# A channel-attention kernel: 47 streamed rows loaded at a later place of the first pass, and 48 others one step earlier

## The chip, the core and the metric

The kernel runs on one core of one Trainium2 chip. The metric is device time in microseconds (us), from the start to the end of one launch. The kernel before was run three times: 720.6, 721.79 and 721.95 us, median 721.79 us. One further execution was recorded by the hardware profiler; it took 720.55 us, and the span from its first to its last instruction is 718.7 us.

The engines are called by their short names: PE (TensorE, matrix products), DVE (VectorE), ACT (ScalarE), POOL (GpSimd), and SP (SyncE, which here only issues DMAs). DMA transfers move rows between HBM, the chip's main memory, and SBUF, the memory that the engines read.

## What is computed

```python
g = jnp.einsum("bhwc->bc", x) / (H * W)      # mean of every channel
gp = jnp.pad(g, ((0, 0), (pad, pad)))        # k = 1, so pad = 0
s = jnp.zeros_like(g)
for i in range(k):
    s = s + gp[:, i:i + C] * w1d[i]
s = _sigmoid(s)
return x * s[:, None, None, :]               # every pixel scaled by its channel's gate
```

`x` is 1 x 384 x 384 x 384 in bfloat16. Seen as pixels by channels that is 147456 x 384. With 128 partitions there are 1152 pixels to a partition; one "row" below is one pixel's 384 channels on each of the 128 partitions, 128 x 384 x 2 = 98304 bytes. The gates depend on all rows, so nothing can be scaled until the last row has been summed: the kernel reads x in a first pass, forms the gates, and writes the scaled x in a second pass.

## The kernel before, in words

**Where rows live.** SBUF holds one buffer, `arena`, of `ROWS` = 275 row slots. The letters in the code are slot numbers: `U` = 108, `G0` = 116, `V` = 212, `A` = 220, `W` = 232, `T` = 259, `Y` = 267. Slots `T` to the end are also the scratch space of the folding described below.

**Three kinds of rows.** Of the 1152 rows, 780 (`N_STREAM`) are *streamed*: loaded, summed, dropped, and loaded again in the second pass. The rest is kept from one pass to the next. 59 of these (`N_RAW`) stay in SBUF as they are; `take_raw` loads them last of all. The others come in *groups* (`GROUPS`): group 9 (`BANKED`) and group 0 (`FIRST`) at the very start, groups 1 to 8 of 32 rows each, and group 10 (`EXTRA`) of 16 rows. The groups are *folded*: four rows are packed into the space of three by placing bits of the fourth in the exponent fields of the other three (`fold`). A fold runs on DVE, with a range check on ACT between its two halves, and it overwrites the rows, so PE must have summed them before. It frees every fourth slot.

**First pass.** For each load SP issues one DMA (`load`, L255), and PE adds each of its rows into one accumulator with one matmul by a matrix of ones (`sum_rows`, issued at L261 or, for the first, at L275). The order is written out by hand: first pieces of up to 48 rows into the slots `EARLY`, with groups 1 and 3 between them, and then the list `BETWEEN`. An entry (g, slots) of it takes group g, folds it, and streams rows into the slots listed. For groups 6 to 8 the entry has two lists: the group comes in three loads of 12, 8 and 12 rows, the first list follows the fold of its first half and the second list the fold of its second half. After group 10 come the raw rows. A piece of over 40 rows in `BETWEEN` is preceded by 16 matmuls on zeros (`keep_warm`).

**What holds a load back.** SP works strictly in order. A load into a slot waits until the previous occupant has been summed by PE (or folded by DVE), and all later loads wait behind it. The class `Flow` derives these waits from the slots that each step reads and writes. The transfers that have already been issued go on meanwhile, in order. I call *lead* of a load the time by which its issue comes before the landing of the load issued just before it: it is the work that the DMA queue still had when SP added to it.

**Between the passes.** When PE has added the 1152nd row, ACT computes the gates (L474) and copies them (L478). Then DVE and POOL scale rows (L486), DVE unpacks the folded ones (L295, L301), SP issues the stores (L498) and, into the slots that come free, loads the streamed rows once more. The order of this second pass is made by a small planner at build time, from its own assumed costs and from the slots, group sizes and number of streamed rows; the lists of the first pass do not enter it.

Of the kernel before, what the change touches and what calls it, by code (L numbers as in the profile page):

```python
# [129 lines left out]
def kernel(  # L130
# [13 lines left out]
    B, H, W, C = x.shape  # L144
# [14 lines left out]
    U = 3 * PIECE + PAIRS * 3 * PAIR  # L159
    G0 = U + PAIR  # L160
    V = G0 + PAIRS * 3 * PAIR
    A = V + PAIR
    N_A = 39
    T = A + N_A
    Y = T + 2 * PIECE
# [12 lines left out]
    EXTRA = len(GROUPS)  # L178
    GROUPS.append((A, PIECE))
    W = A + 3 * PIECE  # L180
# [196 lines left out]
    def stream_all(where, n=None):  # L377
        i = 0
        n = sum(m for _, m in where) if n is None else n
        while n:  # L380
            a, m = where[i % len(where)]
            m = min(n, m)
            stream(m, a)
            n -= m
            i += 1
# [28 lines left out]
    S1, S2, S3 = ([slot] for slot in SLOTS)  # L414

    HIGH = [(A - 48, 48)]
    LOW_COLUMN = [(G0 - 48, 48)]
# [6 lines left out]
    def group(g, where):  # L424

        if isinstance(where, list):
            take(g)
            for k in of_group(g):
                fold(k)
            stream_all(where)  # L430
        else:
            k1, k2 = of_group(g)
            take(g, 0, 12)
            take(g, 24, 32)
            fold(k1)
            stream_all(where[0])
            take(g, 12, 24)
            fold(k2)
            stream_all(where[1])

    BETWEEN = [
        (2, LOW_COLUMN + [(A, 38)]), (4, HIGH),
        (5, [(G0 - 24, 24), (A - 24, 24)] + S1),
        (6, (S2, S3 + S1)), (7, (S2, S3 + S1)),
        (8, (S2 + S1, [(U, 8)] + S3)), (EXTRA, [(W + 4, 8)]),
    ]
    between = sum(n for _, b in BETWEEN for w in b for _, n in (w if isinstance(w, list) else [w]))
    first = N_STREAM - between
# [10 lines left out]
    folding = True  # L459
    for g, where in BETWEEN:  # L460
        group(g, where)
    assert streamed[0] == N_STREAM

    def take_raw(a, n):
        load(raw(a), a, n)
        sum_rows(a, n)

    for a, n in [(U, 8), (W + 12, 15), (V, 8), (W + 4, 8), (W, 4), (T, 8), (Y, 4), (Y + 4, 3), (Y + 7, 1)]:
        take_raw(a, n)
    assert summed[0] == RPP  # L470

# [250 lines left out]
    while True:  # L722

        if dve_at <= now:
# [4 lines left out]
            if landed and (ahead < PENDING or not can):  # L729
                a, at, n, end = landed.popleft()  # L730
# [13 lines left out]
        if alongside and alongside[0][0] <= now:  # L744
            _, a, at, n = alongside.popleft()
            store(at, a, n)
            moves.append([now + LAT, n * ROW + PER_STORE, stored(a, n)])
        while waiting and waiting[0][0] <= now:
            _, n, then, at, a, known = waiting.popleft()
# [12 lines left out]
        if bank_at is None and len(line) <= total - BANKS_AT and got and max(got)[0] >= N_BANKED:  # L762
            a = max(got)[1]
# [11 lines left out]
        if got and todo < N_STREAM:  # L775
            n, a = max(got)
            left = N_STREAM - todo
            left -= run_of(left - 1)[0]
            n = min(n, CAP, left)
# [54 lines left out]
```

## Time and profile before

| quantity | value |
|---|---|
| median of three runs | 721.79 us (720.6 to 721.95) |
| profiled execution | 720.55 us |
| its span | 718.7 us, so 1.85 us lie around it |
| first pass, to the end of the last row's sum | 269.65 us into the span |
| PE, DVE, ACT, POOL busy | 211.5, 485.8, 122.2, 10.2 us |
| DMA | 303.30 MB at a mean of 422 GB/s |

The profile's page divides the span into 40 equal slices of 18 us. In its rows of digits, 9 means 90% or more busy; the row PEclk is the clock granted to PE, in tenths of full speed. Other views are used beside the page. The chain of waits follows the work that ended last back to its start, and lists start, duration and what it was; a DMA in it runs from its issue to its landing. The table of stretches gives, for each stretch of time, its length, the busy time of each engine with the number of instructions in parentheses, then the granted clock, the share of the 16 DMA engines' time and the rate in GB/s. The timeline lists runs of equal instructions with start and duration and, in brackets, the idle time before them and what ended it. The view of one source line gives durations in ns, the start of the first and last instruction, and the time from a DMA's issue to its landing.

### The profile page before, as it was taken

What the parts mean: (1) busy time and instruction counts of PE and PEld (TensorE: products, weight loads), DVE (VectorE), ACT (ScalarE), POOL (GpSimd) and SP (SyncE); (2) the same over time, 40 slices, a digit from 0 to 9 for tenths busy, and PEclk for the clock granted to TensorE, in tenths of its full rate; (3) what the DMA queues carried; (4) which work ended last, traced back from release to release, by engine and by line L of the source; (5) the groups of instructions that cost most, each with busy time, mean ns of one, the idle gap of its engine ahead of it and who ended that gap; (6) DMA issues with size and microseconds to landing.
All of it is one profiled execution on the core that took longest, in us unless ns stands there. A gap on an engine that the chain in (4) does not pass through costs nothing.

```text
span 718.7 us, 2037 instructions
## 1 busy us (share of the span) xinstructions
PE 211.5 (29%) x1186; PEld 0.3 (0%) x3; DVE 485.8 (68%) x454; ACT 122.2 (17%) x101; POOL 10.2 (1%) x7
## 2 busy tenths in 40 slices
PE   4776978987987770000000000000000000000000
PEld 0000000000000000000000000000000000000000
DVE  4606270166789849999997999995991999105640
ACT  3604160144667630000002000000000000000000
POOL 0000000000000005000000000000000000000000
PEclk9998989999999995555555555555555555555555
DMA  9999999999999988999999999999999999999997
GB/s 371 444 428 435 434 429 428 438 431 428 409 428 426 427 353 342 411 425 433 425 434 428 433 435 444 434 420 445 417 447 423 427 448 421 449 427 426 439 425 317
DMA packets 20605, 303.30 MB, mean 422 GB/s; under 512 B 2290, under 2 KB 2674, under 8 KB 8306
## 3 DMA queue, kind: packets, MB, share of 16 engines
q1 hardware_dynamic: 20592, 303.18, 98.9%
q8 instruction: 4, 0.07, 0.0%
q14 instruction: 7, 0.06, 0.0%
q10 hardware_dynamic: 2, 0.00, 0.0%
HBM read 189.92 MB, written 113.25 MB: 422 GB/s over the span
## 4 chain that ended last, share of the span: by engine, by line
DMA 56%; DVE 25%; PE 7%; ACT 3%; another core or an unknown queue 2%; POOL 1%; SPq 1%; issue 0%; DVEq 0%; ACTq 0%
DMA arena<-in_x_dram 40%; DVE arena L486 17%; DMA out_dram<-arena 16%; PE bank L261 7%; DVE arena L295 5%; DVE arena L301 3%; ACT arena L332 2%; POOL arena L486 1%; SPq L255 1%; ACT arena L405 1%; SPq L498 0%; ACT s_bf L474 0%; ACT bank L478 0%; ACT bank L405 0%
## 5 line engine op out<-in xcount | busy, mean ns | idle before, releaser
L486 DVE TENSOR_TENSOR arena<-arena,s_bf 128x1536 bf16<-128x1536 bf16 (+9 forms) x100 | 231.1, 2344 | 78.5 <-DMA arena<-in_x_dram 67.5
L295 DVE TENSOR_SCALAR arena<-arena 128x1536 uint16<-128x1536 uint16 (+3 forms) x240 | 142.9, 644 | 118.6 <-DMA arena<-in_x_dram 101.8
L261 PE MATMUL bank<-arena,ones 128*128 128x384 bf16 x1151 | 205.6, 340 | 49.0 <-DMA arena<-in_x_dram 48.6
L332 ACT ACTIVATE arena<-arena 128x3072 uint16<-128x3072 uint16 (+1 forms) x40 | 108.0, 2699 | 107.7 <-DVE arena L295 107.7
L301 DVE TENSOR_TENSOR arena<-arena 128x1536 uint16<-128x1536 uint16 (+2 forms) x100 | 109.3, 1093 | 7.0 <-PE bank L261 3.1
L556 PE MATMUL bank<-odd,ones 128*128 128x1 bf16 x1 | 0.2, 185 | 313.6 <-DVE odd L551 313.6
L405 ACT COPY arena<-bank 128x512 uint32<-128x512 uint32 (+3 forms) x9 | 4.4, 497 | 106.7 <-DMA out_dram<-arena 106.5
L486 POOL TENSOR_TENSOR arena<-arena,s_bf 128x1536 bf16<-128x1536 bf16 (+1 forms) x3 | 10.0, 3350 | 270.2 <-ACT bank L478 270.2
L405 ACT COPY bank<-arena 128x512 uint32<-128x512 uint32 (+3 forms) x9 | 4.1, 493 | 35.6 <-PE bank L261 35.6
L486 DVE TENSOR_TENSOR arena<-arena,bank 128x1536 bf16<-128x1536 bf16 (+3 forms) x8 | 9.4, 1248 | 0.0
L332 ACT ACTIVATION_READ_ACCUMULATOR arena<-arena 128x1 f32 x40 | 7.5, 186 | 0.0
L261 PE MATMUL bank<-zeros,ones 128*128 128x384 bf16 x32 | 5.5, 326 | 0.0
L275 PE MATMUL bank<-arena,ones 128*128 128x384 bf16 x1 | 0.5, 479 | 7.2 <-DMA arena<-in_x_dram 7.2
L474 ACT ACTIVATE s_bf<-bank,w_sc 128x384 bf16<-128x384 f32 x1 | 0.6, 580 | 8.8 <-PE bank L261 8.8
L802 ACT ACT_TABLE_LOAD x1 | 1.3, 1283 | 0.7 <-PEq L818 0.7
L362 DVE TENSOR_SCALAR w_sc<-bank 128x1 f32<-128x1 f32 x1 | 0.2, 158 | 1.1 <-PE bank L357 1.1
L352 DVE MEMSET ones<- 128x128 bf16 x1 | 0.2, 165 | 1.0 <-SPq L107 1.0
L357 PE MATMUL bank<-w_bf,ones 1*128 1x1 bf16 x1 | 0.2, 179 | 2.1 <-DMA w_bf<-in_w1d_dram 2.1
L560 DVE CAST odd_i<-bank 128x1 int32<-128x1 f32 x1 | 0.2, 157 | 0.3 <-PE bank L556 0.3
L556 PEld LDWEIGHTS bank<-odd,ones 128*128 128x128 bf16 x1 | 0.1, 103 | 573.7 <-DVE odd L551 573.7
L478 ACT COPY bank<-s_bf 128x192 uint32<-128x192 uint32 x1 | 0.3, 323 | 0.0
L546 DVE TENSOR_REDUCE worst<-seen 128x1 f32<-128x40 f32 x1 | 0.2, 189 | 0.0
(8 smaller groups left out, 0.9 us busy)
## 6 DMA issues: line engine op xcount, KB each, us to landing
arena<-in_x_dram SPq DMA_DIRECT2D x17, 4608.0 KB, 29.9
out_dram<-arena SPq DMA_DIRECT2D x9, 3072.0 KB, 24.5
out_dram<-arena SPq DMA_DIRECT2D x5, 4608.0 KB, 35.5
arena<-in_x_dram SPq DMA_DIRECT2D x14, 1152.0 KB, 13.9
arena<-in_x_dram SPq DMA_DIRECT2D x5, 3072.0 KB, 15.2
arena<-in_x_dram SPq DMA_DIRECT2D x6, 2304.0 KB, 18.7
arena<-in_x_dram SPq DMA_DIRECT2D x15, 768.0 KB, 8.9
arena<-in_x_dram SPq DMA_DIRECT2D x2, 4512.0 KB, 29.3
```

The lines of the kernel that those rows point to most:

```text
L255: lambda: nc.sync.dma_start(out=arena[:, a : a + hi - lo, :], in_=view(xf, *run)[:, lo:hi, :]),
L261: return pe.add_instruction(mybir.InstMatmult(name=nc.get_next_instruction_name(), ins=[pe.lower_ap(rhs), pe.lower_ap(ones[:])], outs=[pe. ...
L275: return nc.tensor.matmul(acc, lhsT=ones[:], rhs=arena[:, i, :], start=first, stop=last)
L295: lambda: nc.vector.tensor_scalar(out=dst, in0=src, scalar1=s0, scalar2=s1, op0=op0, op1=op1),
L301: "DVE", lambda: nc.vector.tensor_tensor(out=dst, in0=a, in1=b, op=op), reads=reads, writes=writes
L332: lambda: nc.scalar.activation(out=y, in_=y, func=ACTF.Copy, accum_out=seen[:, 2 * k + i : 2 * k + i + 1]),
L405: "ACT", lambda: nc.scalar.copy(dst.bitcast(u32), src.bitcast(u32)), reads=reads, writes=writes
L474: lambda: nc.scalar.activation(out=s_bf[:], in_=acc, func=ACTF.Sigmoid, scale=w_sc[:, 0:1]),
L478: "ACT", lambda: nc.scalar.copy(s_ps.bitcast(u32), s_bf[:].bitcast(u32)), reads=["s_bf"], writes=["bank0"]
L486: lambda: vec.tensor_tensor(out=v, in0=v, in1=s[:, None, :].to_broadcast([P, n, C]), op=Op.mult),
L556: lambda: nc.tensor.matmul(votes, lhsT=ones[:], rhs=odd[:], start=True, stop=True),
L802: nc.scalar.preload_act_table(ACTF.Sigmoid)
```

## The change

The rows that are streamed, their number (780), the groups, the raw rows and the second pass stay. What is edited is the list of the first pass:

```diff
+    LATE = [(W + 4, 8), (U, 8), (W + 12, 8), (W + 20, 7)]
     BETWEEN = [
-        (2, LOW_COLUMN + [(A, 38)]), (4, HIGH),
-        (5, [(G0 - 24, 24), (A - 24, 24)] + S1),
-        (6, (S2, S3 + S1)), (7, (S2, S3 + S1)),
-        (8, (S2 + S1, [(U, 8)] + S3)), (EXTRA, [(W + 4, 8)]),
+        (2, LOW_COLUMN + HIGH), (4, [(A, 38)]),
+        (5, [(G0 - 24, 24), (A - 24, 24), *S1]),
+        (6, (S2, S3 + S1)), (7, ([(A - 24, 24)] + S2, S3 + S1)),
+        (8, (S2 + S1, [(U, 8)] + S3)), (EXTRA, LATE),
     ]
...
-    for a, n in [(U, 8), (W + 12, 15), (V, 8), (W + 4, 8), (W, 4), (T, 8), (Y, 4), (Y + 4, 3), (Y + 7, 1)]:
+    for a, n in [(V, 8), *LATE, (W, 4), (T, 8), (Y, 4), (Y + 4, 3), (Y + 7, 1)]:
         take_raw(a, n)
```

- `HIGH` (slots 172 to 219, 48 rows) and the 38 rows at `A` change places: `HIGH` now follows group 2 and its streamed `LOW_COLUMN` (slots 68 to 115), and the 38 rows follow group 4.
- Group 7 gets 24 more streamed rows, in slots 196 to 219, which were used for streamed rows after group 5 too.
- After group 10 there are 31 streamed rows, in four loads into the slots `LATE`, where there were 8. The same four slots then take raw rows: `V` (8 rows) is loaded first and then the four slots again, in the same order, so that between the two uses of a slot 31 rows are loaded.
- The raw rows of slots 244 to 258, one load of 15 before, come as 8 and 7.
- `first`, the number of rows streamed ahead of `BETWEEN`, is 780 less the rows in `BETWEEN`: 409 where it was 456. The pieces are 43, 30 and seven of 48, where they were 43, 29 and eight of 48. They take the three slots of `EARLY` so that the last piece is in slots 172 to 219 as before.

SP issues one DMA more. The number of matmuls, 1152 on rows and 32 on zeros, stays.

## The prediction

> **What bounds the kernel now.** I read the page first: the whole span, the slices, the DMA queues.
>
> ```profile
> span 718.7 us, 2037 instructions
> ...
> DMA  9999999999999988999999999999999999999997
> GB/s 371 444 428 435 434 429 428 438 431 428 409 428 426 427 353 342 411 425 433 425 434 428 433 435 444 434 420 445 417 447 423 427 448 421 449 427 426 439 425 317
> ...
> q1 hardware_dynamic: 20592, 303.18, 98.9%
> HBM read 189.92 MB, written 113.25 MB: 422 GB/s over the span
> ```
>
> The DMA row is full everywhere but at the change of passes and at the ends. The kernel is bound by its bytes, and the change moves none of them out: 780 rows are still read twice and 372 once, 1932 x 98304 bytes = 189.9 MB, and 1152 are written. So only time in which the transfers run below their full rate can be won. The table of stretches says how much that is (length, busy times, clock, DMA share, GB/s):
>
> ```profile
> 112.00:180.00 68.00, 57.05 (x328) 0.00 (x0) 27.68 (x38) 20.92 (x16) 0.00 (x0) 0.95 1.00 432
> 194.00:246.00 52.00, 41.54 (x244) 0.00 (x0) 46.20 (x63) 34.89 (x25) 0.00 (x0) 1.00 1.01 427
> 246.00:262.00 16.00, 11.40 (x69) 0.00 (x0) 13.29 (x18) 10.82 (x8) 0.00 (x0) 1.00 1.01 423
> 184.00:186.00 2.00, 2.00 (x15) 0.00 (x0) 1.27 (x2) 0.27 (x1) 0.00 (x0) 1.00 1.03 442
> 186.00:188.00 2.00, 2.00 (x14) 0.00 (x0) 0.63 (x2) 2.00 (x1) 0.00 (x0) 1.00 0.97 387
> 188.00:190.00 2.00, 2.00 (x14) 0.00 (x0) 1.71 (x2) 0.58 (x2) 0.00 (x0) 1.00 0.89 323
> 190.00:192.00 2.00, 2.00 (x15) 0.00 (x0) 2.00 (x6) 0.98 (x1) 0.00 (x0) 1.00 0.94 387
> 192.00:194.00 2.00, 2.00 (x14) 0.00 (x0) 1.84 (x3) 1.88 (x2) 0.00 (x0) 1.00 1.03 442
> 262.00:266.00 4.00, 4.00 (x25) 0.00 (x0) 0.00 (x0) 0.00 (x0) 0.00 (x0) 1.00 0.97 372
> 266.00:270.00 4.00, 2.77 (x17) 0.00 (x0) 0.00 (x0) 0.32 (x1) 0.00 (x0) 1.00 0.29 109
> ...
> 340.00:700.00 360.00, 0.18 (x1) 0.10 (x1) 273.47 (x193) 4.37 (x9) 0.00 (x0) 0.50 1.00 432
> ```
>
> The reader is to see three things. Full rate is 432 GB/s. There is one dent inside the first pass, at 186 to 192 us. And the last loads, from 262 us, run at 372 before the queue drains. From the second pass nothing can be won or lost here: its order is the same instruction for instruction, it begins when the gates are there, and at 432 GB/s with share 1.00 it moves as a block. What the first pass gains at its last sum, the kernel gains.
>
> The chain of waits names both places (start, duration, what):
>
> ```profile
> 74.09 25.69 DMA arena<-in_x_dram
> ...
> 99.82 10.78 PE bank L261 x48
> ...
> 110.61 21.75 DMA arena<-in_x_dram
> ...
> 132.41 7.97 PE bank L261 x48
> ...
> 177.42 9.54 PE bank L261 x48
> ...
> 186.98 9.51 DMA arena<-in_x_dram
> ...
> 260.86 5.98 DMA arena<-in_x_dram
> ...
> 266.88 2.77 PE bank L261 x16
> ```
>
> The first and third rows end at 74.09 + 25.69 = 99.78 and at 132.36; between them three loads of 48 rows land, so a queued row costs 32.58 / 144 = 0.2263 us.
>
> **The dent, which the change removes.** The load issued at 186.98 is the second 24-row load after group 5, slots 196 to 219. It needs the slots of `HIGH`, whose 48 rows landed just before 177.42 and were summed until 186.96. These are the load before it in SP's order, and SP's wait for it:
>
> ```profile
> L255 SPq DMA_DIRECT2D arena<-in_x_dram x1: 328/328/328, 158.6 to 158.6; - x1
> DMA to landing us min/median/max: 31.4/31.4/31.4
> ```
> ```profile
> SPq L255 <- PE bank L261: 28.0, 1, 28.0
> ```
>
> The predecessor lands at 158.6 + 31.4 = 190.0, so the lead is only 3.0 us. The late load lands at 186.98 + 9.51 = 196.5, which is 6.5 us behind it, where 24 queued rows take 24 x 0.2263 = 5.4. It costs 1.0 to 1.1 us. The stretches give a second price: 45, 109 and 45 GB/s below 432 for 2 us each is 398 KB, or 0.9 us. I take 1.0.
>
> After the change `HIGH` is loaded before group 4 and the 38 rows. Between its landing and the end of the predecessor of the same 24-row load lie group 4 (32), 38, group 5 (32) and 24 rows: 126 x 0.2263 = 28.5 us, where it was 56 rows, 12.7 us. Less the sum of `HIGH`, 7.97 to 10.78 us by the rows above, a lead of 17 us or more is left. This term goes: -1.0.
>
> **The late scratch load, which the change removes too.** The raw load of `T` waits until group 10's fold stops using that space:
>
> ```profile
> 258.88 1.94 DVE L301 TENSOR_TENSOR arena<-arena 128x1536 uint16<-128x1536 uint16 x2
> ```
> ```profile
> L255 SPq DMA_DIRECT2D arena<-in_x_dram x1: 328/328/328, 259.0 to 259.0; - x1
> ...
> DMA to landing us min/median/max: 5.8/5.8/5.8
> ```
>
> The fold ends at 260.82, `T` is issued at 260.86; its predecessor, `W`, lands at 259.0 + 5.8 = 264.8. Lead 3.9 us. `T` lands at 266.84, 2.0 to 2.1 us later as 264.8 is rounded, for 8 rows worth 1.8: it costs 0.2 to 0.3, and I take 0.3. What lands behind it costs nothing: PE starts the last 16 rows when `T` is there and needs 2.77 us for them, longer than their remaining 8 rows take on the queue (1.8). So the end of the pass is `T`'s landing plus 2.8 us, before and after. After the change 82 rows land from group 10 to `T` where 59 did, 23 x 0.2263 = 5.2 us more cover for the same fold, and `T` is issued with some 9 us of lead: -0.3. These 23 rows are no addition, as they are gone ahead of `BETWEEN`.
>
> **What it adds.** (1) Smaller loads. 24 of the 47 rows move into a load of 24; 23 move into loads of 7 and 8. By the stretches, large loads run at 432, the stretch of small ones at 423 to 427. 23 rows are 2.26 MB: 5.23 us at 432, 5.35 at 423, so +0.1. The bounds are 0 and, at the 372 of the last loads, +0.85; the stretch 246 to 262, full of 8-row loads, is the nearest row. SP's one more issue of 0.33 us is hidden under the transfers in flight.
>
> [...]
>
> (2) The slots used twice. Each second load must wait for PE's sum of the first. The kernel before has one such load, at slots 236 to 243:
>
> ```profile
> L255 SPq DMA_DIRECT2D arena<-in_x_dram x1: 327/327/327, 257.2 to 257.2; - x1
> ...
> DMA to landing us min/median/max: 6.7/6.7/6.7
> ```
> ```profile
> 253.07 5.36 PE L261 MATMUL bank<-arena,ones 128*128 128x384 bf16 x32 [1.28 <-DMA arena<-in_x_dram]
> ```
>
> There too 31 rows lie between the uses (8 + 15 + 8). The load lands at 257.2 + 6.7 = 263.9. If its 8 rows took the 1.8 us of queued rows, its predecessor landed at 262.1 and its lead was 4.9; the load `W` of 4 rows landing 0.9 us behind it, at 264.8, and no dent in the stretch 246 to 262 bear that out. PE is late there since it first sums group 10's 16 rows, within the row of 32 above. At the three second uses that follow, PE has 8 rows to sum (1.39 us, half of the 2.77 row) while 8 rows, 1.81 us, land: leads of about 5.3, 5.7 and 6.1. Behind each wait stand all later loads, but each lead is above 3.9, the largest that cost anything above. I take 0, with bounds 0 and +0.3 each (`T`'s price).
>
> (3) Other waits that move. `HIGH` now waits for the last 48-row piece ahead of `BETWEEN`; behind that piece are group 2 (32) and `LOW_COLUMN` (48), 18.1 us, less 8 to 10.8 for the sum: lead 7 or more. Group 4 waits for group 2's fold, as before:
>
> ```profile
> 153.67 0.33 SPq L255
> ```
> ```profile
> 159.20 6.34 PE L261 MATMUL bank<-arena,ones 128*128 128x384 bf16 x38 [0.63 <-DMA arena<-in_x_dram]
> ```
>
> There its lead was 159.2 - 153.67 = 5.5 us, with 48 + 38 rows queued behind group 2; now 48 + 48 are, 10 rows or 2.3 us more. If PE sums the piece before at the slow 10.78, it loses 2.8 again: 5.0 at the worst. The 38 rows behind it need a small ACT copy that is done by then. The second 24 rows in group 7 need slots summed some 28 us earlier. All at nothing, covered by those leads. The 16 zero matmuls of `HIGH` go with it, so the clock may halve over the 38 rows after group 4; 1.6 us of PE, under a lead of over 10.
>
> **Sum.** -1.0 - 0.3 + 0.1 = -1.2 us. The profiled execution took 720.55, so 719.35 in its terms. The median of the runs stands 1.24 above that execution; carried over, 721.79 - 1.2 = **720.6 us**, 0.17% less. I count differences within 0.2%, 1.44 us, as not to be told from none.
>
> **The rivals.**
>
> *The dent isn't in every run (small gain).* The sum of `HIGH` took 9.54 us instead of 7.97 because the clock was halved just then, after a gap of 2.99 us in PE's work:
>
> ```profile
> 177.42 18.63 PE L261 MATMUL bank<-arena,ones 128*128 128x384 bf16 x104 [2.99 <-DMA arena<-in_x_dram]
> ```
> ```profile
> 177.00:178.00 1.00, 0.58 (x2) 0.00 (x0) 1.00 (x1) 1.00 (x1) 0.00 (x0) 0.61 1.14 492
> 178.00:179.00 1.00, 1.00 (x5) 0.00 (x0) 0.88 (x3) 0.20 (x2) 0.00 (x0) 0.50 1.03 442
> ...
> 180.00:181.00 1.00, 1.00 (x6) 0.00 (x0) 1.00 (x2) 1.00 (x1) 0.00 (x0) 0.68 0.97 418
> ```
>
> At full clock the lead would be 3.0 + 1.6 = 4.6 us and the dent some 0.1. Then the change brings -0.1 - 0.3 + 0.1 = -0.3: 721.5. Against it: the profiled execution has the dent and is no slower than the fastest run. [...]
>
> *More goes than the dent (larger gain).* Two of the three runs are 1.2 to 1.35 us above the third. If that is one more starved load in the first pass, of the kind that a 3 us lead allows, the longer leads cover it as well, and the median falls to the profiled sum: 720.55 - 1.2 = 719.35. For it: the spread has the size of such a dent. Against: the trace of a fast execution can't show it.
>
> *PE at half clock in the tail (slower).* A half-clock stretch costs PE 9.54 - 7.97 = 1.6 us. The first reload has 4.9 us of lead and a load begins to cost below about 4. With PE late by 1.6 the first reload loses some 0.8, and as the next three are chained to it in PE's order, two such stretches (3.2 us), the second over the last 16 rows where PE sets the end, cost 0.8 + 1.6 = 2.4 and more; with another 0.3 at each of the three later reloads 3.3. 721.79 - 1.2 + 3.3 = 723.9. It decides once PE idles for some 2.5 us there; the gap of 2.99 did it. Against: the gap shown in the tail is 1.28, and the table shows clock 1.00 from 194 to 270 us.
>
> *Small loads at the rate of the last ones.* 0.85 in place of 0.1: 721.3, no difference.
>
> **How the numbers follow.** The forecast has 0.42, the larger gain 0.27, the small gain 0.17, the slower tail 0.10, the slow small loads 0.04. The forecast lies near the bound of 0.2%, 720.35: of its 0.42 I give 0.18 to faster and 0.24 to the same. The small gain gives 0.14 to the same and 0.03 to slower, the slow loads 0.04 to the same. Faster 0.45, same 0.42, slower 0.13. The range reaches to 719.0, below the larger gain, and up to 722.3, which leaves out only most of the slow tail.
>
> **What would show it.** In the changed profile the 24-row load of slots 196 to 219 after group 5 is issued over 15 us ahead of its predecessor's landing, and no stretch of 2 us between 140 and 255 us falls to 323 GB/s. `T` is issued long before `W` lands. The last sum ends near 268.5 us instead of 269.65. The second pass takes as long as before. I am wrong if a reload is issued with under 4 us of lead, if half clock appears after 240 us, or if the first pass ends no earlier.

## The result and the profile after

| | kernel before | changed kernel |
|---|---|---|
| seven runs each | 720.35 to 723.56 us, median 721.79 | 719.49 to 720.15 us, median 719.75 |
| profiled execution | 720.55 us | 720.05 us |
| its span | 718.7 us | 718.3 us |
| last sum of the first pass ends | 269.65 us | 268.76 us |
| from there to the end of the span | 449.1 us | 449.5 us |

The ratio of the times is 0.9974, with a 95% interval of 0.9961 to 0.9986: 0.26% faster. Two later sessions, each with new runs of both kernels, gave 0.9989 (0.9975 to 1.0004) and 0.9989 (0.9977 to 1.0001). The plain mean of the three is 0.9984, or 1.2 us.

The two profiled executions differ by less than the medians, and the runs of the changed kernel lie in a band of 0.7 us where those of before spread over 3.2. That spread turns out to be the subject. In its first pass SP issues four loads more than before, 57 where there were 53, and not one more as I had counted.

First, the page of the changed kernel (span, granted clock, DMA busy tenths, GB/s in 40 slices):

```profile
span 718.3 us, 2042 instructions
...
GB/s 372 443 422 444 434 431 418 447 428 424 428 426 428 425 343 359 413 424 430 425 434 429 433 443 424 435 426 437 434 431 432 443 431 426 436 429 431 447 421 307
```

The eleventh slice, 180 to 198 us, reads 428 where it read 409. The table of stretches of the changed kernel shows the place:

```profile
186.00:188.00 2.00, 2.00 (x15) 0.00 (x0) 2.00 (x5) 1.16 (x1) 0.00 (x0) 1.00 1.00 422
188.00:190.00 2.00, 2.00 (x14) 0.00 (x0) 1.57 (x2) 1.70 (x2) 0.00 (x0) 1.00 1.04 435
190.00:192.00 2.00, 2.00 (x14) 0.00 (x0) 0.96 (x1) 0.50 (x1) 0.00 (x0) 1.00 1.01 425
...
194.00:240.00 46.00, 35.18 (x201) 0.00 (x0) 36.26 (x50) 26.75 (x21) 0.00 (x0) 0.96 1.01 428
```

The dent of 387, 323 and 387 GB/s is gone. The mean clock of 0.96 in the row from 194 to 240 hides a half-clock stretch (0.50 from 214 to 216 us), and the rate there is 428 all the same. The view of the issuing line gives the two 24-row loads after group 5 of the changed kernel, the predecessor first:

```profile
L255 SPq DMA_DIRECT2D arena<-in_x_dram x1: 327/327/327, 148.0 to 148.0; - x1
DMA to landing us min/median/max: 31.4/31.4/31.4
...
L255 SPq DMA_DIRECT2D arena<-in_x_dram x1: 328/328/328, 158.9 to 158.9; - x1
DMA to landing us min/median/max: 26.0/26.0/26.0
```

The predecessor lands at 179.4, so the load that had 3.0 us of lead now has 20.5. The chain of waits of the changed kernel ends the pass as before, with 16 rows behind `T`:

```profile
265.99 2.77 PE bank L261 x16
268.78 0.59 ACT s_bf L475
```

### The profile page after: what moved, and what is told of

It reads as the page before. It is cut to its first block, busy times and chain, and to the rows that moved or that the text cites. A ratio compares the mean times of both kernels' runs of the same rounds, so it can differ in the third digit from the quotient of the medians.

```text
span 718.3 us, 2042 instructions
## 1 busy us (share of the span) xinstructions
PE 213.0 (30%) x1186; PEld 0.3 (0%) x3; DVE 485.6 (68%) x454; ACT 122.1 (17%) x101; POOL 10.2 (1%) x7
## 4 chain that ended last, share of the span: by engine, by line
DMA 54%; DVE 27%; PE 7%; ACT 3%; another core or an unknown queue 2%; POOL 1%; SPq 1%; issue 1%; DVEq 0%; ACTq 0%
DMA arena<-in_x_dram 38%; DVE arena L487 19%; DMA out_dram<-arena 16%; PE bank L261 7%; DVE arena L295 6%; DVE arena L301 3%; ACT arena L332 2%; POOL arena L487 1%; SPq L255 1%; ACT arena L405 1%; SPq L499 0%; ACT s_bf L475 0%; ACT bank L479 0%; ACT bank L405 0%
```

## The experiments

Times are medians; each experiment is compared with runs of the kernel before in the same session.

**The kernel before, again** (unchanged).

> The kernel before, unchanged, for a second profile and more times. Theory A (the loss that the change removes sits in the first pass, at the load that waits for the 48 rows of HIGH, and its size differs between executions with the place of the half-clock stretches of PE): the profile again has a load after group 5 with a lead of 1.5 to 4.6 us, and the end of the last sum lies between 268.8 us (full clock there) and 271 us. Times spread over more than 1.5 us. Rival C (the spread comes from the second pass or from outside the span): last sum within 0.2 us of 269.65 us whatever the time is.

Measured: 721.34 us, 12 runs from 719.52 to 723.01, ratio 0.9999 (0.9984 to 1.0015). The profiled execution was one of 723.01 us. Its stretches and PE's timeline:

```profile
176.00:180.00 4.00, 2.38 (x8) 0.00 (x0) 3.77 (x7) 2.91 (x3) 0.00 (x0) 0.68 0.97 418
...
186.00:188.00 2.00, 2.00 (x15) 0.00 (x0) 0.83 (x2) 2.00 (x1) 0.00 (x0) 1.00 0.90 387
188.00:190.00 2.00, 2.00 (x14) 0.00 (x0) 1.50 (x1) 0.78 (x2) 0.00 (x0) 1.00 0.98 313
190.00:192.00 2.00, 2.00 (x14) 0.00 (x0) 2.00 (x5) 0.76 (x1) 0.00 (x0) 1.00 0.99 406
...
258.00:262.00 4.00, 1.96 (x13) 0.00 (x0) 3.85 (x7) 2.91 (x3) 0.00 (x0) 1.00 0.98 381
262.00:266.00 4.00, 3.77 (x14) 0.00 (x0) 0.36 (x1) 0.46 (x2) 0.00 (x0) 0.60 0.98 382
```
```profile
177.62 18.65 PE L261 MATMUL bank<-arena,ones 128*128 128x384 bf16 x104 [2.93 <-DMA arena<-in_x_dram]
...
262.23 10.13 PE L261 MATMUL bank<-arena,ones 128*128 128x384 bf16 x51 [2.26 <-DMA arena<-in_x_dram]
```
```profile
L255 SPq DMA_DIRECT2D arena<-in_x_dram x1: 328/328/328, 187.2 to 187.2; - x1
DMA to landing us min/median/max: 10.6/10.6/10.6
...
L255 SPq DMA_DIRECT2D arena<-in_x_dram x1: 328/328/328, 253.4 to 253.4; - x1
DMA to landing us min/median/max: 8.8/8.8/8.8
```

The reader sees the same dent after the same gap (2.93 us, 2.99 in the first profile) and half clock (a mean of 0.68 from 176 to 180 us). The late 24-row load, issued at 187.2, again has a lead of 3.1 us, but it lands 7.5 us behind its predecessor where 5.4 are due: 2.1 us late, twice the loss of the first profile. Then comes a second event: at 258 to 262 us the transfers fall to 381 GB/s, the 15-row load issued at 253.4 lands 0.6 us late, PE idles 2.26 us, and the clock is halved over part of its last 51 rows (a mean of 0.60 from 262 to 266 us). They take 10.13 us; at the 0.173 us of the last 16 rows (2.77 / 16) they would take 8.8. The half clock over the last rows is what the prediction feared for the changed kernel's tail, but it is in the kernel before, and no short lead came ahead of it: the 15-row load was issued 4.8 us before its predecessor's landing, as in the first profile (4.9), where it lost nothing. What slowed the transfers at 258 us stays open. The expectation's limit of 271 us was too low: the last sum ended near 272.4. Rival C is out: the gates came 2.7 us later, and from there to the end it took 448.8 us, no longer than in the first profile.

**The exchange alone**, on the kernel before.

```diff
-        (2, LOW_COLUMN + [(A, 38)]), (4, HIGH),
+        (2, LOW_COLUMN + HIGH), (4, [(A, 38)]),
```

> The kernel before with only HIGH and the 38 rows exchanged; tail as before. Theory A: the lead of the 24-row load after group 5 rises from 3.0 to over 15 us, the dent is gone, the late load of T stays; median 1.0 to 1.8 us below the kernel before, and the spread of its runs shrinks below 1 us. Rival B (the gain beyond the dent comes from the tail): median 0.3 to 1.0 us below, spread as before.

Measured: 719.52 us, 718.96 to 721.0, ratio 0.9983 (0.9967 to 0.9999). The median is as expected, the band of 2.0 us wider than that. The dent at 188 us is gone, but the profiled execution shows another:

```profile
124.00:128.00 4.00, 4.00 (x15) 0.00 (x0) 0.00 (x0) 0.00 (x0) 0.00 (x0) 0.54 1.00 433
128.00:130.00 2.00, 2.00 (x15) 0.00 (x0) 0.00 (x0) 0.00 (x0) 0.00 (x0) 1.00 0.85 363
130.00:132.00 2.00, 2.00 (x14) 0.00 (x0) 0.00 (x0) 0.00 (x0) 0.00 (x0) 1.00 0.97 320
...
188.00:190.00 2.00, 2.00 (x14) 0.00 (x0) 1.89 (x2) 2.00 (x1) 0.00 (x0) 1.00 0.99 424
```

Here half clock over the last piece but one ahead of `BETWEEN` (a mean of 0.61 from 120 to 124 us and of 0.54 from 124 to 128) delays the load of group 2, which waits for that piece's first rows (its lead is 4.0 us). At 432 GB/s the two low stretches lose 69 and 112 GB/s for 2 us each, 362 KB or 0.8 us.

**The moved rows alone**: the changed kernel with only the exchange undone (the reverse of that diff).

> The changed kernel with only that exchange undone: the 47 rows stay at their new places. Theory A: the dent is back, as between HIGH and the load that needs its slots lie 56 rows again; median 0.2 to 0.6 us below the kernel before, spread over 1.5 us. Rival B: median 1.2 to 2.0 us below, small spread.

Measured: 721.61 us, 720.51 to 724.51, ratio 1.0015 (0.9998 to 1.0031). No gain, a loss if anything, where theory A had 0.2 to 0.6 us of gain: its dent came back, but that alone would only have left the time of before. In its stretches the dent is back, and a second one, at group 4's load, has joined it:

```profile
144.00:148.00 4.00, 4.00 (x26) 0.00 (x0) 3.84 (x7) 2.90 (x4) 0.00 (x0) 1.00 0.89 329
...
178.00:180.00 2.00, 2.00 (x14) 0.00 (x0) 0.84 (x1) 1.34 (x2) 0.00 (x0) 1.00 0.95 304
```
```profile
122.17 10.75 PE L261 MATMUL bank<-arena,ones 128*128 128x384 bf16 x48 [3.13 <-DMA arena<-in_x_dram]
```

The timeline's row is PE on the last piece ahead of `BETWEEN`: 10.75 us for 48 rows that take 7.97 at full clock (the row at 132.41 us in the first profile of before). What follows is late by that: the sum of group 2, its fold, and the load of group 4, which waits for the fold.

**More zeros ahead of `HIGH`**, on the kernel before: the order of loads stays, only PE's gap is filled.

```diff
-            keep_warm(N_WARM)
+            keep_warm(30 if a == A - 48 else N_WARM)
```

> The kernel before with 30 zero matmuls ahead of HIGH in place of 16, so that PE's gap ahead of the 48 rows shrinks from 3.0 to about 0.6 us. If the half clock makes the dent: clock 1.00 over the 48 rows, their sum 8.0 us instead of 9.5, lead of the 24-row load about 4.6 us, dent 0.1 us; median 0.5 to 1.2 us below the kernel before. If the short distance of 56 rows alone makes it: lead still 3 us, time unchanged.

Measured: 719.95 us, 719.11 to 720.87, ratio 0.9986 (0.9974 to 0.9997). PE's timeline, the stretches, and the 24-row load with its predecessor:

```profile
177.75 17.06 PE L261 MATMUL bank<-arena,ones 128*128 128x384 bf16 x104 [0.71 <-DMA arena<-in_x_dram]
```
```profile
176.00:180.00 4.00, 3.29 (x21) 0.00 (x0) 3.77 (x7) 2.91 (x3) 0.00 (x0) 1.00 1.00 430
...
188.00:190.00 2.00, 2.00 (x14) 0.00 (x0) 1.88 (x4) 0.91 (x2) 0.00 (x0) 1.00 1.01 424
```
```profile
L255 SPq DMA_DIRECT2D arena<-in_x_dram x1: 327/327/327, 185.7 to 185.7; - x1
DMA to landing us min/median/max: 10.1/10.1/10.1
...
L255 SPq DMA_DIRECT2D arena<-in_x_dram x1: 328/328/328, 158.9 to 158.9; - x1
DMA to landing us min/median/max: 31.5/31.5/31.5
```

The gap is 0.71 us, the clock stays at 1.00, the 104 rows take 17.06 us instead of 18.63, the lead is 190.4 - 185.7 = 4.7 us, and there is no dent. So 56 rows of distance suffice at full clock, and the half clock is what spends them.

**No zeros ahead of `HIGH`**, on the kernel before (the same line with 0 for 30).

> The kernel before without the 16 zero matmuls ahead of HIGH; LOW_COLUMN keeps its own. PE then idles about 5.7 us ahead of the 48 rows. Theory A: half clock for 3.4 to 6.8 us over them, their sum takes 9.6 to 11.2 us, the lead of the 24-row load after group 5 falls to 1.4 to 3.0 us and it loses 1.0 to 3 us; median 0.3 to 2 us above the kernel before. If the zeros don't matter: sum and time as before.

Measured: 722.49 us, six runs from 721.19 to 723.25, ratio 1.0024 (1.0007 to 1.0041). PE's timeline and the stretches:

```profile
177.81 24.51 PE L261 MATMUL bank<-arena,ones 128*128 128x384 bf16 x135 [5.55 <-DMA arena<-in_x_dram]
```
```profile
176.00:180.00 4.00, 2.19 (x7) 0.00 (x0) 3.77 (x6) 2.90 (x3) 0.00 (x0) 0.50 0.99 427
...
188.00:192.00 4.00, 4.00 (x27) 0.00 (x0) 2.48 (x3) 0.98 (x2) 0.00 (x0) 1.00 0.85 304
```

A gap of 5.55 us, half clock behind it, and 304 GB/s for 4 us: 128 GB/s under 432, 512 KB or 1.2 us. With the last experiment this moves the kernel's time both ways by nothing but PE's gap.

**The changed kernel, again** (unchanged, in two sessions).

> The changed kernel, for a second profile and more times. Theory A (short lead and half clock together made the losses): no load between 140 us and the end of the first pass loses more than 0.5 us, wherever the half-clock stretches lie; last sum ends between 268.4 and 269.6 us; median 1.0 to 2.0 us below the kernel before of the same session, all runs within 1.5 us. Rival (the gain was chance of the first session): median within 0.5 us of before.

> The changed kernel once more, for that comparison: 0.7 to 2.0 us below the median of the kernel before, narrow spread, fastest runs no faster than the fastest of before.

Measured: 720.37 us (719.93 to 721.57) and 720.21 us (719.67 to 720.81), with the ratios given at the top. The medians lie 1.15 and 0.66 us below those of before, the second a little short of the expected 0.7; one band is 1.64 us wide where 1.5 was expected. The gates came at 269.11 and 269.25 us, and no load between 140 us and the end of the pass lost 0.5 us.

**The exchange alone, again**, beside the second of these.

> The exchange of HIGH and the 38 rows alone, once more, beside the changed kernel in one session. If the 47 moved rows are worth nothing on top of the exchange, as theory A has it (the late load of T costs 0.3 us at most): within 0.5 us of the changed kernel. Rival B (the moved rows matter too): 0.7 us or more above it.

Measured: 720.17 us (719.5 to 721.59), 0.04 us from the changed kernel. The 47 moved rows add nothing that can be measured. Its load of `T`, preceded by that of `W`, still comes late:

```profile
L255 SPq DMA_DIRECT2D arena<-in_x_dram x1: 327/327/327, 260.3 to 260.3; - x1
DMA to landing us min/median/max: 5.8/5.8/5.8
...
L255 SPq DMA_DIRECT2D arena<-in_x_dram x1: 328/328/328, 258.5 to 258.5; - x1
DMA to landing us min/median/max: 5.8/5.8/5.8
```

`W` lands at 264.3, `T` at 266.1: 1.8 us for 8 rows, all that they must take, at a lead of 4.0 us by these rounded rows. The late `T` is free here.

**Second uses closer together**, on the changed kernel: 23 rows between them.

```diff
-    for a, n in [(V, 8), *LATE, (W, 4),
+    for a, n in [*LATE, (V, 8), (W, 4),
```

> The changed kernel with the raw rows of V loaded behind the four second uses, so that 23 rows lie between the two uses of a slot, not 31. If a lead under 4 us costs by itself: the first second use is issued with a lead of about 3.1 us and lands 1 to 2 us late; the last sum ends 1 to 2 us later than in the changed kernel, and the median is 0.8 to 2 us above it. If only the half clock makes a short lead cost, at full clock nothing is lost here and the time is that of the changed kernel.

Measured: 721.68 us (720.85 to 722.41), ratio 1.0000 (0.9982 to 1.0018), 1.3 us above the changed kernel of the same session. The first second use, then the stretches with clock and rate, then PE's timeline at the load before it:

```profile
L255 SPq DMA_DIRECT2D arena<-in_x_dram x1: 328/328/328, 252.6 to 252.6; - x1
DMA to landing us min/median/max: 6.0/6.0/6.0
```
```profile
254.00:256.00 2.00, 1.83 (x11) 0.00 (x0) 1.97 (x3) 2.00 (x1) 0.00 (x0) 1.00 0.81 298
256.00:258.00 2.00, 0.91 (x6) 0.00 (x0) 0.26 (x1) 0.34 (x2) 0.00 (x0) 1.00 0.97 289
```
```profile
255.62 1.30 PE L261 MATMUL bank<-arena,ones 128*128 128x384 bf16 x7 [0.17 <-DMA arena<-in_x_dram]
```

PE starts the 7 rows of the predecessor at 255.6, as they land, so the lead is 3.0 us. The load lands at 258.6, 3.0 us behind, where 8 rows take 1.8: it costs 1.2 us, at a clock of 1.00. So here a lead of 3.0 us cost 1.2 us at full clock; in the two profiles of before the lead of 3.0 and 3.1 us came with half clock, which is one way to get it. The margin of the second uses in the changed kernel is needed.

The profile is of this kernel's slowest run, 722.41 us, and holds another late load, which the order of the second uses does not touch:

```profile
214.40 18.25 PE L261 MATMUL bank<-arena,ones 128*128 128x384 bf16 x94 [3.95 <-DMA arena<-in_x_dram]
```
```profile
L255 SPq DMA_DIRECT2D arena<-in_x_dram x1: 327/327/327, 229.4 to 229.4; - x1
DMA to landing us min/median/max: 7.3/7.3/7.3
```

PE idles 3.95 us until the 24 rows of group 7 land, then runs at half clock (0.50 from 214 to 220 us). The 12-row load that waits for a part of these sums is issued with a lead of 3.7 us and lands 0.9 us late.

**`T` in two loads**, on the changed kernel.

```diff
-(W, 4), (T, 8), (Y, 4),
+(W, 4), (T, 4), (T + 4, 4), (Y, 4),
```

> The changed kernel with the 8 raw rows of T loaded as 4 and 4. PE can sum the first four while the next land, so that the last sum no longer ends 2.8 us behind the landing of all eight: the end comes 0.4 to 0.5 us nearer to the last landing (0.45 us behind it in place of 0.89). Median 0 to 0.5 us below the changed kernel. Rival: PE is not what ends the pass, and nothing moves.

Measured: 720.12 us (719.67 to 720.64) against 720.37: lower by 0.25, not to be told apart. PE's timeline ends so:

```profile
266.37 2.42 PE L261 MATMUL bank<-arena,ones 128*128 128x384 bf16 x12 [0.20 <-DMA arena<-in_x_dram]
```

The gap of 0.84 us ahead of 16 rows became one of 0.20 ahead of 12: the direction is right, the effect below what the runs resolve.

**Zeros for the last pieces too.** Ahead of each of the last three pieces before `BETWEEN` stand 16 zero matmuls, and `T` is split, once on the exchange alone and once on the changed kernel.

```diff
+        if i >= len(sizes) - 3:
+            keep_warm(N_WARM)
         stream_all([EARLY[(i - len(sizes)) % 3]], n)
```

> The exchange alone, with 16 zero matmuls ahead of each of the last three pieces before BETWEEN, and T loaded as 4 and 4. Theory A: the half clock at about 121 us, which left group 2 a lead of 4.0 us, is gone; lead 5 us or more there; last sum ends between 267.8 and 268.8 us; median 0.3 to 1.0 us below the exchange alone, both kernels beaten. Rival: zeros that meet no gap delay PE by 2.8 us, the lead of group 2 falls and the time rises by 0.5 us or more.

> The same two edits on the changed kernel: as its lead at group 2 is larger (5.0 to 7.0 us), the zeros win less: median 0.2 to 0.6 us below the changed kernel, from the split of T for the most part.

Measured: 720.08 us (719.06 to 720.55) and 719.95 us (719.5 to 721.12), beside 720.17 and 720.21 without. In the first, the clock was 1.00 from the landing of group 2 to 262 us:

```profile
140.00:262.00 122.00, 100.78 (x600) 0.00 (x0) 96.67 (x130) 74.42 (x53) 0.00 (x0) 1.00 1.01 428
```

Neither beats the kernel that it was built on by what the runs can tell, and the first misses its expected 0.3 us. Group 2's load had a lead of 5.2 us there, against 4.0 and 6.7 in the two profiles of the exchange alone: the zeros take half clock away (a mean of 0.93 from 92 to 140 us, 0.89 in the first profile of before), but they delay PE too (16 of them take 2.76 us in that profile). With them nothing more that can be measured is won once the exchange is made.

## Why the prediction held, and where it did not

**The place was right, and its size is not one number.** The dent cost 1.0 us in the execution that I had, and 2.1 in the other profile of before, with a second loss behind it. In other executions it is small or absent, as the times suggest and no profile shows: the fastest run of before, 718.91 us, is as fast as any kernel here. What makes it differ between executions was not shown. Over all four sessions 61 of 117 runs of the kernel before took over 721 us; of 30 runs of the changed kernel 2 did, of 24 of the exchange alone 1, of 12 with longer zeros none, of 6 without zeros all 6, of 12 with the moved rows alone 9. The change does not make a good execution faster. It makes the bad half rare.

**The number.** I carried the 1.2 us of one profile over to the medians, as if the other runs of before were that execution plus 1.24 us. They are not: the changed kernel has no such offset, its profiled execution is 0.3 us above its median. The first session's medians differ by 2.0 us, nearer to the larger gain (719.35) than to the forecast, the later two by 1.15 and 0.66. That the mean of the three ratios comes to the forecast's 1.2 us is in part luck. In the terms of the profiled execution the forecast was 719.35, and 720.05 was measured: the last sum came 0.9 us earlier and not 1.2, and the second pass took 0.4 us longer.

**The rivals.** I gave the small gain, "the dent isn't in every run", 0.17, and spoke against it with the profiled execution being no slower than the fastest of three runs. That argument failed: three runs were too few to show an execution without the dent. The larger gain had 0.27 for "one more starved load" of the kind that a 3 us lead allows; the second profile shows a larger loss at the same load and one more at 258 us, but that one without a short lead. With 30 zeros ahead of `HIGH` in one run (gap 0.71 us, clock 1.00, no dent) and none in another (gap 5.55 us, clock 0.50, 1.2 us lost), the cause of the dent is shown, not only argued; the cause of the loss at 258 us is not.

**The exchange.** A lead of 17 us or more was predicted, 20.5 was measured, and the exchange alone brings the whole gain.

**The late `T`, -0.3: mis-sized.** With the same late issue `T` costs nothing measurable in the profiles of the exchange alone, of the longer zeros and of no zeros; the 0.3 of the first profile wasn't the price of its lead, and what made it stays open. In the changed kernel `T` had 7.7 us of lead, not some 9. The last sum moved by 0.9 us, which fits the dent's 1.0 less 0.1 for the small loads, and not by 1.2; in the two later profiles it ended 0.6 and 0.4 us earlier than in the first of before.

**The small loads, +0.1.** In the changed kernel the stretch from 194 to 240 us runs at 428 GB/s, where 427 was read before: nothing dearer appeared, and the rate of the last ones, 372, was no price for these. SP's further issues, four and not one, cost nothing either: from 240 us to the end of the pass no load lands over 0.1 us late.

**The slots used twice.** I predicted a lead of 4.9 us. By the view of the issuing line in the changed kernel, its first second use is issued at 251.1 and its predecessor at 246.2:

```profile
L255 SPq DMA_DIRECT2D arena<-in_x_dram x1: 328/328/328, 251.1 to 251.1; - x1
DMA to landing us min/median/max: 6.7/6.7/6.7
...
L255 SPq DMA_DIRECT2D arena<-in_x_dram x1: 430/430/430, 246.2 to 246.2; - x1
DMA to landing us min/median/max: 9.8/9.8/9.8
```

The predecessor lands at 256.0, lead 4.9 us, and 8 rows follow in 1.8. The three after it have leads of 5.4, 5.6 and 6.0, where 5.3, 5.7 and 6.1 were predicted. The step was right, and the run with 23 rows between the uses shows what it would have cost otherwise.

**The other waits, at nothing: right for two, incomplete for the third.** `HIGH` has 8.8 us of lead (7 or more predicted) and group 4 6.4 (5.0 at the worst). The 24 rows added to group 7 cost nothing at their own load, which has 16.3 us of lead, though their slots were summed some 3 us ahead of the issue and not some 28. But they come as one load, for which PE idles 3.9 us, and half clock follows in each of the three profiles of the changed kernel (0.50 from 214 to 216 us in the first). The prediction had no such gap. The 12-row load that waits for the sums behind it has leads of 5.2, 4.8 and 4.1 us there and loses 0.1 at most; in the run with 23 rows it had 3.7 and lost 0.9. So the change leaves one thin place of its own.

**The slower tail** (0.10) did not come in any profile of the changed kernel; the half clock did come elsewhere, within 194 to 240 us. The 2.5 us of idle time that I gave as its condition was my estimate (in the first profile of before the clock behind a gap of 1.98 us, at 150.6 us, is 1.00, and behind one of 2.89 us, at 121.6, it falls to 0.50), and it is no limit: in the second profile of before 2.26 us were enough. Nor does the length of a gap decide: in two profiles of the changed kernel a gap of 2.69 us stands ahead of the 38 rows after group 4, and the clock behind it is 1.00 in one and 0.57, from 168 to 172 us, in the other.

**The second pass "moves as a block": not quite.** From the gates to the end it took 449.1 us before and 449.5 after, which is why the spans differ by 0.4 us only. Over all 14 profiles this time lies between 448.8 and 449.9 us, with no order by kernel that I can see, while the last sum ends anywhere from 268.4 to 272.4. So the spread comes from the first pass for the most part. What varies in the second is open; no run was made for it.

## What to carry to other kernels

In a kernel whose transfers are the bound, look for waits by the lead that each load has when it is issued, and not for idle time: a lead of 3.0 to 3.1 us cost 0.8 to 2.1 us in each of the four profiles that had one. If PE can fall to half clock, allow for it in the distance between two uses of a buffer (here it made the sum of 48 rows 1.6 us longer, 9.54 for 7.97), or keep PE busy across the gap ahead of the work that a load waits for (30 zeros left a gap of 0.71 us here, and the clock stayed at 1.00). And look at the spread of the runs before sizing a term from one trace: the loss at one load was 1.0 us in one profile of before and 2.1 in the other, and with it gone 2 of 30 runs took over 721 us where 61 of 117 had.

## What the runs showed that I had not expected

- A lead does not have one price. About 4 us cost nothing at `T` (8 rows, 1.8 us) and about 0.8 us at group 2 in the exchange alone, where 32 rows follow a 48-row load; 3.1 us at the dent cost 1.0 us in one profile of before and 2.1 in the other. And one stretch of 2 us is a poor witness: in the changed profile 142 to 144 us reads 336 GB/s, and no load lands late around it.
- A load can land late without a short lead. At 258 us in the second profile of before it was 0.6 us at 4.8 us of lead, and with no zeros two loads issued 11 and 15 us ahead landed 0.9 and 0.4 us late, at 219 and 221 us, some 30 us after the dent. Whether a starved queue passes its loss on to them was not tried.
- The moved rows without the exchange made group 4's load late (329 GB/s over 4 us: 412 KB under 432, 0.95 us). The step that gives it stands in the prediction, for the changed kernel: with the piece ahead summed at half clock (10.78 us), group 4's lead of 5.5 us loses 2.8, and only the exchange adds 2.3. Without it 2.7 are left; 2.6 were measured. I had not carried the step over to this experiment. The profile shows the slow sum, 10.75 us, and the load's issue at 146.2 us, which in the kernel waits for the fold; a run with full clock there was not made.
